# A fused recurrent attention and gated FFN: first v load in two halves, k and q ahead of v for two chunks, one attention block and its casts two groups later

## The chip, the cores and the metric

One core of a Trainium2 chip. The time is device microseconds (us) of one execution; most executions agree within a few tenths of a per cent, and the kernel before measured 230.6 to 232.7 us over four sets of rounds. "Faster" and "slower" mean a difference of more than 2%.

## The reference, cut to what matters

```python
gamma = 1.0 - 2.0 ** (-5.0 - np.arange(H))            # B, H, S, D = 4, 8, 768, 64
for t in range(S):
    state = gamma * state + k[t] outer v[t]            # per batch and head, 64 x 64
    y[t]  = scale * q[t] @ state
x   = y as (B*S, H*D)                                  # 3072 x 512
out = (sigmoid(x @ w_gate) * (x @ w_val)) @ w_out      # d_ff = 1536
```

## The kernel before

The sequence is cut in chunks of 128 tokens (six for each batch, 24 in all), and the recurrence becomes masked scores within a chunk plus a carried state. 512 tokens of x at a time then go through the FFN: 12 "up" groups (gate and value columns, the product into hT) and 8 "down" groups. In the second 512 tokens, where the change works, groups 0 to 7 are up groups for the first 256 tokens (each two sets of four matmuls of 128x256), and the "column groups" after them do the same for the other 256. Groups are counted from 0. Attention work for later chunks is put between the groups by a plan: after group i, do this step.

Chunks 0 to 3 are loaded as two runs of 256 tokens, k and q cast to bf16 by GpSimd's DMA, the first v by SyncE's:

```python
def load_run(x, a, dtype, eng, name):
    t = const.tile([128, H, 2 * D], dtype, name=name, tag=name, bufs=1)
    eng.dma_start(out=t, in_=x[0, :, a * 2 * C:(a + 1) * 2 * C, :].rearrange("h (p j) d -> p h (j d)", j=2))
    return t
vr[0] = load_run(v, 0, F32, nc.sync, "vr")
nc.scalar.preload_act_table(AX.Exp)
kr[0] = load_run(k, 0, BF16, nc.gpsimd, "kr0")
# ... qr[0], kr[1], qr[1] on GpSimd, later vr[1] on GpSimd, the weights, then chunks 4 to 9
```

Chunks 4 to 7 are transposed on TensorE (`step_t`: transposes, a ScalarE copy to qkT, VectorE's scaling of v). From chunk 8 on, SyncE transposes by DMA (qkX), and GpSimd's loads of chunks 10 and 11 wait for qkX of 8.

```python
def block(done, new):        # cut to its parts; new: the two chunks whose scores start; done: the two that are finished
    # inter(done): q @ carried state; scores(new); intra(done); state(new)   -- TensorE
    # y_out(done), masks(new), state_sum(new)                                -- VectorE
def casts(g):                # the carried state of g, g+1 to bf16           -- ScalarE
plan = {
    0: [(9, step_t, 4), (10, step_t, 5), (11, block, None, 4), (12, step_t, 6), (13, casts, 4), (13, step_t, 7),
        (14, block, 4, 6), (15, scale_v, 8)],
    1: [(0, casts, 6), (2, scale_v, 9), (4, block, 6, 8), (6, casts, 8), (10, scale_v, 10), ...,
        (12, block, 8, 10), ...],
# ... cut
```

Names in the profile lines: kn, qn, vf are a chunk's loads and vs the scaled v (kr, qr, vr, vsr for the runs of 256); za is the carried state and zbd its bf16 copy; ff is an accumulator of TensorE, gs the sigmoid, ob an output.

Each engine runs its instructions in program order, so a step also holds up what stands behind it on its engine.

Of the kernel before, what the change touches and what calls it, by code (L numbers as in the profile page):

```python
# [9 lines left out]
F32 = mybir.dt.float32  # L10
BF16 = mybir.dt.bfloat16
# [6 lines left out]
def kernel(  # L18
# [10 lines left out]
    nc = tc.nc  # L29
    B, H, S, D = q.shape  # L30
    N_TOK, D_MODEL = out.shape
    D_FF = moe_w_gate.shape[1]
    C = 128
# [25 lines left out]
    def load_v(g):  # L59
        vf[g] = ld.tile([C, H, D], F32, tag="vf", name="vf", bufs=6)  # L60
        nc.gpsimd.dma_start(out=vf[g], in_=src(v, g))  # L61

    def load_kq(g):
        kn[g] = ld.tile([C, H, D], BF16, tag="kn", name="kn")
        qn[g] = ld.tile([C, H, D], BF16, tag="qn", name="qn")
        nc.gpsimd.dma_start(out=kn[g], in_=src(k, g))  # L66
        nc.gpsimd.dma_start(out=qn[g], in_=src(q, g))  # L67

    def load_chunk(g):
        load_kq(g)  # L70
        load_v(g)


    def load_run(x, a, dtype, eng, name):
        t = const.tile([128, H, 2 * D], dtype, name=name, tag=name, bufs=1)
        eng.dma_start(out=t, in_=x[0, :, a * 2 * C:(a + 1) * 2 * C, :].rearrange("h (p j) d -> p h (j d)", j=2))
        return t

    wg = wpool.tile([128, KT, D_FF], BF16, name="wg")
# [9 lines left out]
    def load_out(s):  # L89
        nc.gpsimd.dma_start(out=wo[:, s * 3:(s + 1) * 3, :],  # L90
                            in_=moe_w_out.rearrange("(n p) d -> p n d", p=128)[:, s * 3:(s + 1) * 3, :])


    kr, qr, vr, vsr = {}, {}, {}, {}
    vr[0] = load_run(v, 0, F32, nc.sync, "vr")
    nc.scalar.preload_act_table(AX.Exp)
    kr[0] = load_run(k, 0, BF16, nc.gpsimd, "kr0")
    ident = const.tile([128, 128], BF16, name="ident")
    make_identity(nc, ident)
    ident4 = ident.unsqueeze(1).to_broadcast([128, 4, 128])  # L100
# [1 line left out]
    nc.gpsimd.iota(tokr, pattern=[[2 * C, 2], [1, 2]], base=0, channel_multiplier=2)  # L102
    tokv = const.tile([128, NCH], I32, name="tokv")
    nc.gpsimd.iota(tokv, pattern=[[C, NCH]], base=0, channel_multiplier=1)
    qr[0] = load_run(q, 0, BF16, nc.gpsimd, "qr0")
    toky = const.tile([128, 384], I32, name="toky")
    nc.gpsimd.iota(toky, pattern=[[1, 384]], base=0, channel_multiplier=0)
    kr[1] = load_run(k, 1, BF16, nc.gpsimd, "kr1")
    qr[1] = load_run(q, 1, BF16, nc.gpsimd, "qr1")

    lgh = const.tile([128, H], F32, name="lgh")
    for h in range(H):
# [39 lines left out]
    def bank(shape, dt=F32):  # L152
        return pf.tile(shape, dt, tag="ff", name="ff")
# [122 lines left out]
    def scale_run(a, eng):  # L276
        vsr[a] = const.tile([128, H, 2, D], BF16, name=f"vsr{a}")
        eng.tensor_tensor(vsr[a], runs(vr[a]), tabr[:, a].unsqueeze(3).to_broadcast([128, H, 2, D]), op=ALU.mult)  # L278
# [173 lines left out]

    make_taby(0)
    scale_run(0, nc.vector)
    vr[1] = load_run(v, 1, F32, nc.gpsimd, "vr")
    maskr = const.tile([128, 2, 2, D], F32, name="maskr")
    nc.gpsimd.memset(maskr, 1.0)
    for i in range(2):
# [51 lines left out]
    extend_taby(5)  # L510
    for s in range(4):
        load_out(s)
    for g in range(4, 8):
        load_chunk(g)
    y[3] = bank([128, NP, C])
    intra_run(1, [3])
    y_out_run(2)
# [15 lines left out]
    def downs(t):  # L533
# [2 lines left out]
    plan = {  # L536
        0: [(9, step_t, 4), (10, step_t, 5), (11, block, None, 4), (12, step_t, 6), (13, casts, 4), (13, step_t, 7),
            (14, block, 4, 6), (15, scale_v, 8)],
        1: [(0, casts, 6), (2, scale_v, 9), (4, block, 6, 8), (6, casts, 8), (10, scale_v, 10), (11, scale_v, 11),
            (12, block, 8, 10), (14, casts, 10), (16, scale_v, 12), (17, scale_v, 13), (20, block, 10, 12),  # L540
            (22, casts, 12)],
        2: [(3, scale_v, 14), (4, scale_v, 15), (6, block, 12, 14), (8, casts, 14), (11, scale_v, 16),
# [69 lines left out]
```

## Time and profile before

| | before |
|---|---|
| time, median of the first 3 runs | 231.94 us |
| span of the profiled run | 229.3 us |
| TensorE / VectorE / ScalarE / GpSimd busy | 96 / 51 / 38 / 34% |
| granted TensorE clock | 1.0 |
| TensorE idle in the span | 9.4 us, 3.0 of them before its first matmul |

TensorE is the bound, and only holes in its work can be won. "Idle before" in a profile line gives the time the engine stood and what ended it. Since ends of matmuls are modelled, starts are the surer reading. The lines are in the prediction.

I use five marks, 0 (the start of the span) and four starts on TensorE: B, the block of chunks 4 to 6; C, the first up group of the second 512 tokens; D, the block of chunks 8 to 10; E, the last matmul. Before: B 50.07, C 53.29, D 72.26, E 225.89 us.

### The profile page before, as it was taken

The numbers are of one execution on the slowest core, as the hardware profiler recorded it, in microseconds if no ns is written. First come the engines' busy times: TensorE is split into PE (matmuls) and PEld (weight loads), VectorE is DVE, ScalarE is ACT, GpSimd is POOL, SyncE is SP. The second block draws the span as 40 slices with busy tenths as digits, with TensorE's granted clock in tenths as the row PEclk, the third lists the DMA queues.
The fourth block names the chain that finished last, engine by engine and source line by source line (L and its number), as shares of the span: only waits on it lengthen the run. The fifth ranks groups of instructions, "written<-read, shape, count | busy, mean of one in ns | idle before, by whom it ended". The sixth has DMA issues, their size and how long they took to land.

```text
span 229.3 us, 4531 instructions
## 1 busy us (share of the span) xinstructions
PE 219.9 (96%) x1815; PEld 119.1 (52%) x1815; DVE 117.9 (51%) x224; ACT 87.0 (38%) x162; POOL 78.9 (34%) x106
## 2 busy tenths in 40 slices
PE   4879999999899999999999999999999999999994
PEld 1557544567687445445445445445445454444443
DVE  5586433459876927368626267637267520343301
ACT  5785332554362421632521532623432512433221
POOL 7899956740724417080620090810000000000000
PEclk9999999999999999999999999999999999999999
DMA  7999999999897999799792399992420012100022
GB/s 136 219 189 196 198 206 196 186 242 194 108 190 60 164 149 175 191 129 171 61 192 94 92 137 160 94 165 88 105 40 0 0 49 91 46 0 0 4 91 92
DMA packets 77653, 28.08 MB, mean 122 GB/s; under 512 B 64192, under 2 KB 73280, under 8 KB 77632
## 3 DMA queue, kind: packets, MB, share of 16 engines
q0 software_dynamic: 55440, 16.78, 65.3%
q1 hardware_dynamic: 22048, 10.95, 23.8%
q8 instruction: 14, 0.23, 0.4%
q10 hardware_dynamic: 144, 0.07, 0.1%
q14 instruction: 7, 0.06, 0.1%
HBM read 28.31 MB, written 6.29 MB: 151 GB/s over the span
## 4 chain that ended last, share of the span: by engine, by line
PE 84%; DMA 10%; POOL 2%; issue 1%; DVE 1%; SPq 1%; DVEq 0%
PE ff L386 47%; PE ff L422 23%; PE ff L404 5%; DMA kn<-in_k_dram 4%; DMA wv<-in_moe_w_val_dram 3%; PE ff L232 2%; PE ff L183 2%; DMA vr<-in_v_dram 2%; DMA qkX<-qn 2%; PE ff L195 1%; PE ff L441 1%; PE z L201 1%; DVE vsr L278 1%; SPq L169 1%; PE ff L162 0%
## 5 line engine op out<-in xcount | busy, mean ns | idle before, releaser
L393 DVE TENSOR_TENSOR hT<-gs,ff 128x512 bf16<-128x512 f32 (+1 forms) x70 | 44.8, 648 | 59.1 <-PE ff L386 53.4
L386 PE MATMUL ff<-xT,wg 128*128 128x512 bf16 (+1 forms) x280 | 67.6, 364 | 0.2 <-DVE hT L393 0.2
L386 PE MATMUL ff<-xT,wv 128*128 128x512 bf16 (+1 forms) x280 | 67.6, 364 | 0.1
L392 ACT ACTIVATE gs<-ff 128x512 f32<-128x512 f32 (+1 forms) x70 | 39.5, 567 | 67.7 <-PE ff L386 61.7
L422 PE MATMUL ff<-wo,hT 128*128 128x512 bf16 x276 | 62.2, 379 | 0.0
L386 PEld LDWEIGHTS <-wv 128*128 128x128 bf16 x280 | 27.3, 98 | 29.3 <-DMA wv<-in_moe_w_val_dram 0.3
L422 PEld LDWEIGHTS <-hT 128*128 128x128 bf16 x276 | 26.3, 98 | 30.5
L386 PEld LDWEIGHTS <-wg 128*128 128x128 bf16 x280 | 26.9, 98 | 28.3 <-issue 0.4
L427 ACT COPY ob<-ff 128x512 f32<-128x512 f32 x23 | 13.5, 585 | 49.2 <-PE ff L422 45.1
L250 DVE TENSOR_TENSOR xT<-ff,taby 128x512 bf16<-128x512 f32 x20 | 12.9, 686 | 22.7 <-PE ff L232 22.7
L553 POOL COPY gate<-qkX 1x1 bf16<-1x1 bf16 x7 | 1.6, 234 | 59.0 <-DMA qkX<-qn 59.0
L66 POOL DMA_DIRECT2D kn<-in_k_dram x20 | 17.9, 894 | 5.8 <-DMA qkX<-kn 1.5
L207 ACT CAST zbd<-za 64x256 bf16<-64x256 f32 x38 | 15.3, 403 | 10.1 <-DVE za L219 4.8
L67 POOL DMA_DIRECT2D qn<-in_q_dram x20 | 18.0, 899 | 2.7 <-DMA wo<-in_moe_w_out_dram 1.6
L61 POOL DMA_DIRECT2D vf<-in_v_dram x20 | 18.4, 918 | 1.5 <-DMA wo<-in_moe_w_out_dram 1.0
L174 DVE TENSOR_TENSOR vs<-vf,tabv 128x512 bf16<-128x512 f32 x20 | 13.6, 686 | 6.8 <-DMA vf<-in_v_dram 6.8
L188 DVE TENSOR_TENSOR stA<-ff,causal 128x512 bf16<-128x512 f32 x20 | 13.6, 681 | 0.0
L189 DVE TENSOR_TENSOR stB<-ff,causal 128x512 bf16<-128x512 f32 x20 | 13.6, 680 | 0.0
L404 PE MATMUL ff<-xT,wg 128*128 128x256 bf16 x56 | 7.3, 273 | 1.1 <-DMA wg<-in_moe_w_gate_dram 1.1
L433 PE MATMUL ff<-ident 128*128 128x512 bf16 x15 | 5.3, 494 | 3.0 <-POOL ident masks.py:199 3.0
L404 PE MATMUL ff<-xT,wv 128*128 128x256 bf16 x56 | 7.3, 273 | 0.1
L411 DVE TENSOR_TENSOR hT<-gs,ff 128x512 bf16<-128x512 f32 x7 | 4.7, 687 | 4.0 <-PE ff L404 3.9
(86 smaller groups left out, 150.0 us busy)
## 6 DMA issues: line engine op xcount, KB each, us to landing
out_dram<-ob SPq DMA_DIRECT2D x23, 256.0 KB, 2.1
vf<-in_v_dram POOLq DMA_DIRECT2D x20, 256.0 KB, 5.5
kn<-in_k_dram POOLq DMA_DIRECT2D x20, 128.0 KB, 4.9
qn<-in_q_dram POOLq DMA_DIRECT2D x20, 128.0 KB, 5.7
wg<-in_moe_w_gate_dram POOLq DMA_DIRECT2D x6, 256.0 KB, 7.6
wv<-in_moe_w_val_dram POOLq DMA_DIRECT2D x6, 256.0 KB, 8.3
wo<-in_moe_w_out_dram POOLq DMA_DIRECT2D x4, 384.0 KB, 10.1
vr<-in_v_dram SPq DMA_DIRECT2D x1, 512.0 KB, 4.2
```

The lines of the kernel that those rows point to most:

```text
L61: nc.gpsimd.dma_start(out=vf[g], in_=src(v, g))
L66: nc.gpsimd.dma_start(out=kn[g], in_=src(k, g))
L67: nc.gpsimd.dma_start(out=qn[g], in_=src(q, g))
L174: nc.vector.tensor_tensor(vs[g], vf[g], tabv[:, g % NCH, :].unsqueeze(2).to_broadcast([C, H, D]), op=ALU.mult)
L188: nc.vector.tensor_tensor(stA[g], sc[g][0], causal4, op=ALU.mult)
L189: nc.vector.tensor_tensor(stB[g], sc[g][1], causal4, op=ALU.mult)
L207: nc.scalar.copy(zbd[g % 4][half, :, half], z[half])
L386: nc.tensor.matmul(u[:, lo:hi], w[:, kk, n1 * 128:(n1 + 1) * 128], x_cols(t, kk, lo, hi), start=(kk == 0), stop=(kk == KT - 1))
L392: nc.scalar.activation(gs[:, lo:hi], ps[0][:, lo:hi], AX.Sigmoid)
L393: nc.vector.tensor_tensor(hT[t][:, n1, lo:hi], gs[:, lo:hi], ps[1][:, lo:hi], op=ALU.mult)
L404: nc.tensor.matmul(u[:, i * n:(i + 1) * n], w[:, kk, n1 * 128:(n1 + 1) * 128], x_cols(t, kk, lo, hi), start=(kk == 0 and (rows == 1 or i = ...
L422: nc.tensor.matmul(o, hT[t][:, n1, sm * 128:(sm + 1) * 128], wo[:, n1, :], start=(n1 == 0), stop=(n1 == NFF - 1))
```

## The change

The intent: get the first v sooner by splitting its load over two issuing engines; let q of chunk 7 land before v of 6 so that TensorE needn't wait for it; and move the block of 6 to 8 to a place where its DMA transposes have landed, with the casts of 6 behind two more sigmoids.

```diff
+            eng.dma_start(out=t[:, i * n:(i + 1) * n], in_=runs[:, i * n:(i + 1) * n])   # for each engine
...
-    vr[0] = load_run(v, 0, F32, nc.sync, "vr")
+    vr[0] = load_run(v, 0, F32, "vr", nc.sync, nc.scalar)
...
-    for g in range(4, 8):
-        load_chunk(g)
+    load_chunk(4)
+    load_chunk(5)
+    for load in (load_kq, load_v):
+        load(6)
+        load(7)
...
-        1: [(0, casts, 6), (2, scale_v, 9), (4, block, 6, 8), (6, casts, 8), (10, scale_v, 10), (11, scale_v, 11),
+        1: [(2, casts, 6), (3, scale_v, 9), (6, block, 6, 8), (9, casts, 8), (10, scale_v, 10), (11, scale_v, 11),
```

More of the change, by code (lines that the diff above doesn't have):

```diff
@@ L71, in load_chunk, with load_run @@
         load_v(g)
-    def load_run(x, a, dtype, eng, name):
+    def load_run(x, a, dtype, name, *engines):
         t = const.tile([128, H, 2 * D], dtype, name=name, tag=name, bufs=1)
-        eng.dma_start(out=t, in_=x[0, :, a * 2 * C:(a + 1) * 2 * C, :].rearrange("h (p j) d -> p h (j d)", j=2))
+        runs = x[0, :, a * 2 * C:(a + 1) * 2 * C, :].rearrange("h (p j) d -> p h (j d)", j=2)
+        n = H // len(engines)
+        for i, eng in enumerate(engines):
+            eng.dma_start(out=t[:, i * n:(i + 1) * n], in_=runs[:, i * n:(i + 1) * n])
         return t
@@ L94 @@
     kr, qr, vr, vsr = {}, {}, {}, {}
-    vr[0] = load_run(v, 0, F32, nc.sync, "vr")
+    vr[0] = load_run(v, 0, F32, "vr", nc.sync, nc.scalar)
     nc.scalar.preload_act_table(AX.Exp)
-    kr[0] = load_run(k, 0, BF16, nc.gpsimd, "kr0")
+    kr[0] = load_run(k, 0, BF16, "kr0", nc.gpsimd)
     ident = const.tile([128, 128], BF16, name="ident")
@@ L104 @@
     nc.gpsimd.iota(tokv, pattern=[[C, NCH]], base=0, channel_multiplier=1)
-    qr[0] = load_run(q, 0, BF16, nc.gpsimd, "qr0")
+    qr[0] = load_run(q, 0, BF16, "qr0", nc.gpsimd)
     toky = const.tile([128, 384], I32, name="toky")
     nc.gpsimd.iota(toky, pattern=[[1, 384]], base=0, channel_multiplier=0)
-    kr[1] = load_run(k, 1, BF16, nc.gpsimd, "kr1")
-    qr[1] = load_run(q, 1, BF16, nc.gpsimd, "qr1")
+    kr[1] = load_run(k, 1, BF16, "kr1", nc.gpsimd)
+    qr[1] = load_run(q, 1, BF16, "qr1", nc.gpsimd)
     lgh = const.tile([128, H], F32, name="lgh")
@@ L454 @@
     scale_run(0, nc.vector)
-    vr[1] = load_run(v, 1, F32, nc.gpsimd, "vr")
+    vr[1] = load_run(v, 1, F32, "vr", nc.gpsimd)
     maskr = const.tile([128, 2, 2, D], F32, name="maskr")
```

## The prediction

> **What bounds the kernel now.** I read the first two parts of the page (busy shares, the 40 slices), then TensorE's waits, then the chain of waits, then the order in time of TensorE, ScalarE, GpSimd and SyncE between 40 and 75 us, and last the packet and landing records of the DMA queues.
>
> ```profile
> PE 219.9 (96%) x1815; PEld 119.1 (52%) x1815; DVE 117.9 (51%) x224; ACT 87.0 (38%) x162; POOL 78.9 (34%) x106
> ...
> DMA  7999999999897999799792399992420012100022
> ```
>
> TensorE is busy in 219.9 of 229.3 us at full granted clock, so at most 9.4 us can be won, and 3.0 of those pass before its first matmul. The DMA line is near full to slice 15, about 86 us, then thins. So the change works on a few small holes in the first third. TensorE's own waits name them:
>
> ```profile
> PE ff L433 <- POOL ident masks.py:199: 3.0, 1, 3.0
> PE ff L404 <- DMA wg<-in_moe_w_gate_dram: 1.1, 1, 1.1
> PE ff L183 <- DMA qkX<-qn: 0.6, 1, 0.6
> PE ff L162 <- DMA qn<-in_q_dram: 0.3, 1, 0.3
> PE ff L386 <- DVE hT L393: 0.2, 1, 0.2
> ```
>
> The last three are the target of parts two and three. In order of time around the block of chunks 6 to 8:
>
> ```profile
> 48.54 0.40 PE L162 MATMUL ff<-ident,qn 128*128 128x128 bf16 x4 [0.31 <-DMA qn<-in_q_dram]
> ...
> 57.14 0.60 PE L386 MATMUL ff<-xT,wg 128*128 128x256 bf16 x4 [0.20 <-DVE hT L393]
> 57.84 0.60 PE L386 MATMUL ff<-xT,wv 128*128 128x256 bf16 x4
> 58.27 0.39 PE L195 MATMUL ff<-qkT,zbd 128*128 128x128 bf16 x4
> 58.71 0.40 PE L183 MATMUL ff<-qkX 64*128 64x128 bf16 x8
> 59.68 0.40 PE L183 MATMUL ff<-qkX 64*128 64x128 bf16 x8 [0.57 <-DMA qkX<-qn]
> ```
>
> Starts matter more than the bracketed idle, because ends are modelled. Undisturbed, a set of four 128x256 matmuls starts every 0.436 us (54.60, 55.03, 55.47 in the trace), the first part of the block takes 0.22 and each set of scores 0.27. The starts above are late by 0.36 (57.14; the set before started at 56.34), 0.26, 0.22 and 0.70: 1.54 us lost here, not the 0.8 that the brackets show. The first two losses have one cause:
>
> ```profile
> 55.73 1.65 ACT L207 CAST zbd<-za 64x256 bf16<-64x256 f32 x4 [1.36 <-DVE za L217]
> 57.40 1.31 ACT L392 ACTIVATE gs<-ff 128x256 f32<-128x256 f32 x4
> ```
>
> ScalarE stands at the casts of chunk 6 from 54.37 until za is there, and the sigmoids of groups 1 to 4 queue behind; TensorE lacks a free accumulator.
>
> **What the Trainium skill says.** "DMA: Bandwidth & Descriptors", section "Issuing engines are not separate DMA queues": DMAs from several engines run on the same 16 engines and interleave; starting them on several engines only saves sequencer time. The trace agrees in part. From 3.0 to 4.0 us v alone moves about 67 packets of 512 B per 0.1 us at 27 ns each, which is all 16 engines. But from 1.9 to 2.9 it moves only 12 to 19 per 0.1 us, so the engines starve and a second issuer might help there. Section "Queues, rings and completion order" of that page: each engine goes round-robin between rows, a whole packet of at most 64 descriptors at a time. v is 1024 packets, 64 for each engine, and kr (issued at 1.32) starts only as v ends: its first packets appear at 4.0 and its rate rises from 9 to 65 per 0.1 us while v's falls from 62 to 7. That fits a kr held behind v, though it does not prove it.
>
> **The change part by part.**
>
> **1. v in two halves.** Chain and GpSimd suggest that v matters:
>
> ```profile
> 0.81 4.23 DMA vr<-in_v_dram
> ...
> 6.65 0.89 POOL vr L76
> ...
> 9.55 6.55 DMA wv<-in_moe_w_val_dram
> ```
>
> The tempting reading is that v sooner frees GpSimd's next issue sooner (it idles 0.48 us for vsr), hence the weights sooner. I don't believe it: GpSimd's queue is full already. Its landings follow each other with no hole: kr 6.79, qr 8.22, kr 9.72, qr 11.21, second v 12.86, first wg 14.94, wv 16.10, then one 256 KB weight piece per 1.3 us. The second v is issued at 6.65 but its packets run only from about 10 to 11.6. An earlier issue just queues longer. (Only the first v is split, the second stays with GpSimd.) Nor does TensorE wait for vsr: it is done at 6.37 and first used at 7.40. What remains is a kr that starts sooner because v ends sooner. If two issuers double the slow start, about 170 more of the 1024 packets are moved by 2.9 us, worth 170/67 x 0.1 = 0.25 us at the full rate. The whole GpSimd queue would move by that, and with it TensorE, which waits for wg until 14.98 and for wv until 16.15. ScalarE has room: its table load ends at 2.09 and its next work is at 3.92. Estimate 0 to 0.4, taken as 0.2 us.
>
> **2. k, q of 6, 7 before v.** The number of issues and bytes is unchanged. q of chunk 7 landed at 48.49, after v of 6; as fourth rather than fifth of these six it lands about one piece (1 us) sooner, and TensorE's 0.31 us at 48.54 goes. v of 6 lands at about 48.3 instead of 46.13; VectorE then scales it by 49.1, still before v of 7 (49.45, scaled 50.2), and the state matmuls need both only at 51.6. Gain 0.31 us.
>
> **3. Casts and block later.** With the casts behind group 2 instead of group 0, ScalarE does the sigmoids of groups 1 and 2 before za is ready: the 0.26 goes. The 0.36 stays, since VectorE reaches hT of group 0 only at 56.67. The block then comes behind groups 5 and 6, which take 1.75 us together; TensorE reaches its scores at about 60.0, when qkX has landed (the last at 59.54): 0.22 and 0.70 go. One edge: groups 8 on read the second half of xT, which the block's y_out writes. By my count y_out ends near 62.05 and group 8 is reached at 62.2, so it just fits. About 0.1 us of other hitches is ignored. Gain 1.54 - 0.36 = 1.18, about 1.2 us.
>
> Sum on TensorE at 62 us: 0.2 + 0.31 + 1.2 = 1.7 us.
>
> **What is given back.** The next block reads the transposed q of chunk 11:
>
> ```profile
> 68.37 2.07 SPq L169 DMA_TRANSPOSE qkX<-qn  x1
> ...
> 72.26 0.61 PE L195 MATMUL ff<-qkX,zbd 128*128 128x128 bf16 x8
> 72.81 0.40 PE L183 MATMUL ff<-qkX 64*128 64x128 bf16 x8
> ```
>
> That transpose lands at 71.94. Its scores start near 72.97 (72.26 + 0.44 + 0.27), so the slack is about 1.0 us. The chain behind it (qkX of 8 landed 58.58, GpSimd's gate, loads of 10 and 11 from 59.15, transposes) hangs on the DMA queues, not on TensorE, so parts 2 and 3 don't bring it forward; part 1 would. Of the 1.5 us of parts 2 and 3 I expect 0.9 to 1.5 to survive: 0.5 is lost to a new wait at chunk 11's scores unless the transposes happen to run faster. They well may: both groups of transposes stall about 1.2 us (57.0 to 58.2, 69.5 to 70.5), each time just after a 16 KB instruction fetch of over 1 us, which moves with TensorE's progress. I take 1.05. From there on TensorE has no wait worth naming, so what is ahead stays ahead.
>
> **Rivals.** (a) All hidden: the 1.5 us is fully given back at the block of chunks 8 to 10, and v's split does nothing: 231.9. For it: the thin slack; against: the slack is positive, so about 1 us must survive. (b) The chain of waits is right and v's issue sets the weights: up to 0.5 us for GpSimd plus all of parts 2 and 3, nothing given back: about 229.9. Against: the gapless landings. (c) A new wait: v halves delay kr by taking two turns to its one, or VectorE's burst after the later block holds the column groups or casts of 8: 232 to 232.8. Against: v moves the same bytes, kr starts after it anyway, and the accumulators that the column groups need are freed about 0.2 us or more ahead.
>
> **Range and chances.** 0.2 + 1.05 = 1.25 us off 231.94 is 230.7. The three timed runs spread over 0.6 us, about as wide as the doubt about v (0.4) and about the giving back (0.6), so 229.8 to 231.8 should hold eight times in ten. Two per cent would be 4.6 us: no hole this change touches is that large, in either direction.
>
> **What would show it.** Right: no wait of TensorE at the transposes of 7 nor at the block of 6 to 8; that block starts near 59.5; kr's first packets and landing a little before 4.0 and 6.79; a new wait of up to 0.7 us, or none, at chunk 11's scores near 71 to 72. Wrong: kr's landing unmoved or later (part 1), a wait at the column groups for xT (part 3), or a block of 8 to 10 at the old time, which would leave nothing.

## The result, and the profile after

Median 229.89 us (229.68 to 230.38, 6 runs) against 231.30 us for the kernel before (230.77 to 232.09, 6 runs). Ratios here are the mean time of one kernel's fast runs over that of the other's of the same rounds, so not quite the ratio of the medians: 0.9937, 95% interval 0.9914 to 0.9960, or 1.46 us less between the means. By the 2% rule that is "the same"; by the interval it is a real gain of about 0.6%.

First the busy shares and the DMA line of the page after:

```profile
PE 220.3 (97%) x1815; PEld 119.4 (52%) x1815; DVE 117.9 (52%) x224; ACT 87.4 (38%) x162; POOL 78.6 (34%) x106
...
DMA  7999999999999999899892499992410012100022
```

The work is the same; only the span is shorter, 228.0 for 229.3 us. TensorE's waits after (us in total, times, longest):

```profile
PE ff L436 <- POOL ident masks.py:199: 3.0, 1, 3.0
PE ff L407 <- DMA wg<-in_moe_w_gate_dram: 0.7, 1, 0.7
PE ff L269 <- DMA qr<-in_q_dram: 0.4, 1, 0.4
PE ff L407 <- DMA wv<-in_moe_w_val_dram: 0.3, 1, 0.3
```

The waits for q of 7, for qkX and for hT are gone from this list. Those for the first loads and weights remain. (The kernel before also had three short waits in the first 13 us, for kr and stB, that the prediction's list leaves out.) In order of time around the moved block (start us, us):

```profile
48.55 0.39 PE L165 MATMUL ff<-ident,qn 128*128 128x128 bf16 x4
...
50.61 0.85 PE L186 MATMUL ff<-qkT 64*128 64x128 bf16 x16
...
57.01 0.60 PE L389 MATMUL ff<-xT,wg 128*128 128x256 bf16 x4
57.44 0.60 PE L389 MATMUL ff<-xT,wv 128*128 128x256 bf16 x4
...
59.63 0.39 PE L198 MATMUL ff<-qkT,zbd 128*128 128x128 bf16 x4
59.95 0.67 PE L186 MATMUL ff<-qkX 64*128 64x128 bf16 x16
```

From C (53.51) every start follows in the undisturbed step of 0.437 us, through all seven groups into the block. The scores of 6 and 7 at 50.61, though, took 0.85 us. In the kernel before the same line took 0.62, which is 0.23 us less:

```profile
50.61 0.62 PE L183 MATMUL ff<-qkT 64*128 64x128 bf16 x16
```

That is a new wait; experiment 2 comes back to it. ScalarE in the same stretch:

```profile
55.96 0.39 ACT L395 ACTIVATE gs<-ff 128x256 f32<-128x256 f32 x1 [0.49 <-PE ff L389]
56.37 1.65 ACT L210 CAST zbd<-za 64x256 bf16<-64x256 f32 x4
58.04 0.94 ACT L395 ACTIVATE gs<-ff 128x256 f32<-128x256 f32 x3
```

It does the sigmoid of group 2 first, and the casts no longer wait for za. At the block of 8 to 10, where the prediction expected something to be given back:

```profile
67.84 1.19 SPq L172 DMA_TRANSPOSE qkX<-qn  x1
...
71.05 0.61 PE L198 MATMUL ff<-qkX,zbd 128*128 128x128 bf16 x8
71.59 0.62 PE L186 MATMUL ff<-qkX 64*128 64x128 bf16 x16
```

No wait, but only just: the transposed q of 11 landed at 71.66 us, and its scores started at 71.83, 0.17 us later. Where TensorE did wait for such a transpose (before and experiments 1, 2, 5, 7 and 10), it started 0.13 to 0.14 us after the landing, so the slack was about 0.03 us. The moved block itself had none: q of 9 landed at 60.08, its scores started at 60.22, 0.27 us behind those of 8 where 0.23 is undisturbed (experiment 3). It still lost about 0.04 us. At the start of the kernel the chain of waits reads almost as before:

```profile
0.81 4.19 DMA vr<-in_v_dram
...
6.60 0.89 POOL vr L79
...
9.51 6.87 DMA wv<-in_moe_w_val_dram
```

By the marks, before against after: 0 to B 50.07 and 50.06 us; B to C 3.22 and 3.45; C to D 18.98 and 17.54; D to E 153.63 and 153.63. The gain of the profile, 1.21 us, is the 1.44 won between C and D less the 0.23 lost between B and C; from D on nothing changed by as much as 0.01 us. Inside the first stretch two things cancel: the first full up group started 0.28 us later (24.29 for 24.01), and the way from there to B was 0.29 us shorter.

### The profile page after: what moved, and what is told of

Same layout as the page of the kernel before. It is cut to its first block, busy times and chain, and to the rows that moved or that the text cites. A ratio compares the mean times of both kernels' runs of the same rounds, so it can differ in the third digit from the quotient of the medians.

```text
span 228.0 us, 4533 instructions
## 1 busy us (share of the span) xinstructions
PE 220.3 (97%) x1815; PEld 119.4 (52%) x1815; DVE 117.9 (52%) x224; ACT 87.4 (38%) x162; POOL 78.6 (34%) x106
## 4 chain that ended last, share of the span: by engine, by line
PE 90%; DMA 5%; POOL 1%; ACT 1%; DVE 1%; issue 0%; DVEq 0%
PE ff L389 50%; PE ff L425 26%; PE ff L407 5%; DMA wv<-in_moe_w_val_dram 3%; PE ff L235 2%; PE ff L186 2%; DMA vr<-in_v_dram 2%; PE ff L198 1%; PE ff L444 1%; PE z L204 1%; PE ff L165 1%; DVE vsr L281 1%; ACT qkT L167 0%; POOL vr L79 0%; POOL maskr L463 0%; ACT zbd L210 0%
## 5 line engine op out<-in xcount | busy, mean ns | idle before, releaser
L436 PE MATMUL ff<-ident 128*128 128x512 bf16 x15 | 5.8, 532 | 3.0 <-POOL ident masks.py:199 3.0
```

## The experiments

Experiments 1 to 4 ran on one chip in one set of rounds; 5 to 12 ran on another chip, in three sets. Each set had its own runs of the kernel before, but 12 shares those of 9 to 11 and adds one. Means below are of 5 or 6 runs against 11 or 12.

**1. Only v in two halves (e1_v_split).**

```diff
-    vr[0] = load_run(v, 0, F32, nc.sync, "vr")
+    vr[0] = load_run(v, 0, F32, "vr", nc.sync, nc.scalar)
```

> Only v of the first two chunks in two halves. Theory A (v's end moves kr only a little, and the GpSimd queue's own pace hides it): kr's first packets up to 0.2 us earlier, its landing within 0.2 us of the kernel before, time within 0.3 us of it. Theory B (the chain through v sets the first weights): wg lands 0.3 to 0.5 us sooner and the time falls by 0.3 to 0.5 us. Theory C (the halves disturb the queue, as the profile of the whole change could suggest, where wg and wv land 0.07 and 0.28 us later than before): time up by 0.2 to 0.4 us.

Measured: ratio 0.9985 (0.9968 to 1.0003), 0.30 us less and not clear of nothing. The packet records explain why little can come of it (packets that started in each 0.1 us, by issuer):

```
us      before, SyncE    halves: SyncE  ScalarE
2.1          19                45         0
2.5          18                11         0
2.9          37                40        26
3.5          70                29        37
last v     4.41 us            4.30 us
first kr   4.00 us            3.95 us
```

ScalarE's half was issued at the same time (0.81 us), but its first packet came at 2.78 us, 0.85 after SyncE's; from 3.0 both share the rate that one had. v ends 0.1 us sooner and kr starts 0.05 us sooner. Two profiles can mislead here, so take all: by 3.0 us the three with the split (after, 1, 9) had started 275 to 328 packets, the ten with v in one piece by SyncE 179 to 281, with means of 302 and 217. That lead of 85 packets ends v about 0.1 us sooner (last packets at 4.28 to 4.38 against 4.36 to 4.53 us), but kr's first packet (3.85 to 3.95 against 3.81 to 4.08) and its landing (6.51 to 6.71 against 6.22 to 7.42) are not sooner beyond their scatter. Theory A holds for the mechanism. B's landings of the weights did not show: wg landed at 15.78 us, later than the 14.94 of before. The cause of that is elsewhere: the sixteenth completion of the second k came at 11.46 us, 1.27 us after the fifteenth. Such a late last part came and went from profile to profile, with and without the split (0.02 to 1.39 us among thirteen profiles), so C is not shown by it either.

**2. Only k, q of 6 and 7 before v (e2_kq_order).**

```diff
-    for g in range(4, 8):
-        load_chunk(g)
+    load_chunk(4)
+    load_chunk(5)
+    for load in (load_kq, load_v):
+        load(6)
+        load(7)
```

> Only k, q of chunks 6, 7 ahead of their v. Theory A (the wait for q of 7 goes, but ScalarE's copy of the transposes of 7 stands behind an output copy and the casts of 4, so the scores of 7 wait in its place): no wait at the transposes of 7, a wait of about 0.2 us at the scores of 7, and less than 0.15 us of the 0.31 us kept; at the block of 6 to 8 that gain is lost again, because it waits for the transposes from the DMA, so the time is within 0.2 us of before. Theory B (the hole is simply removed): time down by 0.3 us.

Measured: ratio 0.9976 (0.9958 to 0.9994), 0.57 us less between the means. Its profile shows the first part of theory A; first TensorE, then ScalarE, in order of time:

```profile
48.26 0.39 PE L162 MATMUL ff<-ident,qn 128*128 128x128 bf16 x4
...
50.32 0.84 PE L183 MATMUL ff<-qkT 64*128 64x128 bf16 x16
```
```profile
48.24 0.59 ACT L427 COPY ob<-ff 128x512 f32<-128x512 f32 x1 [0.27 <-PE ff L422]
48.85 0.82 ACT L207 CAST zbd<-za 64x256 bf16<-64x256 f32 x2
49.69 1.02 ACT L164 ACTIVATE qkT<-ff 128x1024 bf16<-128x1024 bf16 x1
```

No wait at the transposes of 7; but their copy by ScalarE stands behind an output copy and the casts of 4 and ends at 50.71, while TensorE reached the scores of 7 at 50.59. They start 0.22 us late (B to C 3.44 for 3.22). What the order wins is the old hole minus 0.22 us. The old hole itself varies with how the start of the kernel went. The next transposes of q of 7 come 1.74 us after those of 6 if nothing waits, and came after 2.22, 1.91, 2.02, 2.30, 1.74 and 1.85 us in the six profiles with the old order (before, 1, 3, 5, 6, 7). The second part of A (all lost at the next block) did not hold: C to D was 18.74, 0.24 us less than before, since the transposes of 9 landed at 59.23 for 59.54. But experiment 1, with the old order and the old plan, had 18.55 there, so that 0.24 can't be put down to the order. By the profiles the order is worth 0 to 0.3 us, and the 0.57 of the totals, with an interval of 0.14 to 0.97, doesn't settle it further.

**3. Only the plan (e3_plan).**

```diff
-        1: [(0, casts, 6), (2, scale_v, 9), (4, block, 6, 8), (6, casts, 8), (10, ...
+        1: [(2, casts, 6), (3, scale_v, 9), (6, block, 6, 8), (9, casts, 8), (10, ...
```

> Only the later casts and the block of 6 to 8 two groups later. Theory A (this part is nearly the whole gain): no wait in TensorE from the first up group of the second 512 tokens to the block of 8 to 10, the distance from the start of that first group to the start of the block of 8 to 10 falls from 18.97 us to about 17.5, time down by 1.2 to 1.5 us. Theory B (half of the gain or more is due to the other two parts): time down by 0.7 us or less, with a wait left at the block.

Measured: ratio 0.9926 (0.9908 to 0.9944), 1.67 us less; C to D 17.49 us, no wait between them. Theory A: this part alone gives what the whole change gives.

**4. The whole change without the split (e4_no_v_split).** The edits of 2 and 3 together.

> The whole change without the split of v. Theory A (the split is worth nothing): time equal to the whole change within 0.2 us, that is 1.2 to 1.7 us below before. Theory B (the split is worth 0.2 to 0.5 us): only 0.9 to 1.2 us below before. Theory C (the split costs): 1.7 us or more below before.

Measured: ratio 0.9917 (0.9897 to 0.9938), 1.87 us less; C to D 17.50, B to C 3.44. That is theory C's range by the number, but only 0.2 us below the plan alone, within the noise. The split is not needed for the gain; whether it costs was left to 9 and 10.

**5. Only the casts of 6 later (e5_casts_only), the block in its old place.**

```diff
-        1: [(0, casts, 6), (2, scale_v, 9), (4, block, 6, 8), (6, casts, 8), (10, ...
+        1: [(2, casts, 6), (3, scale_v, 9), (4, block, 6, 8), (6, casts, 8), (10, ...
```

> Only the casts of 6 (and the scaling of v of 9) later, the block of 6 to 8 where it was. Theory A (two causes in a row; with the first removed TensorE only comes to the second sooner): the late starts of the fourth up group of the second 512 tokens (0.36 and 0.26 us) are gone, but the scores of the block wait that much longer for the transposes of 8 and 9, whose landing does not move: 1.3 to 2 us of waiting there, time within 0.3 us of before. Theory B (the casts alone are most of the gain): time down by 0.6 us or more.

```profile
56.94 0.60 PE L386 MATMUL ff<-xT,wg 128*128 128x256 bf16 x4
57.38 0.60 PE L386 MATMUL ff<-xT,wv 128*128 128x256 bf16 x4
57.82 0.39 PE L195 MATMUL ff<-qkT,zbd 128*128 128x128 bf16 x4
58.13 0.67 PE L183 MATMUL ff<-qkX 64*128 64x128 bf16 x8
59.88 0.40 PE L183 MATMUL ff<-qkX 64*128 64x128 bf16 x8 [1.08 <-DVE hT L393]
```

The late starts are gone, the block is reached 0.61 us sooner after C (4.37 for 4.98 us), and the second set of scores starts 1.48 us later than it could (59.88 for 58.13 + 0.27). C to D: 19.02 us, against 18.98 before. All 0.61 us are given back, as theory A said. The profile puts the wait down to VectorE's hT, which ended near the same time; but q of 9 landed at 59.74, 0.14 before the start, and in the kernel before at 59.54, 0.14 before its start, so the transposes would have held it there in any case. In all five profiles with the block in its old place (before, 1, 2, 5, 7) the scores of 9 start 0.13 to 0.14 us after that landing. The total is 0.44 us less (ratio 0.9975, 0.9954 to 0.9997), more than the 0.3 expected; in the profile, which is of the slowest of the six runs (231.17 us), that difference isn't between C and D, and its cause stays open.

**6. Only the block later (e6_block_only), the casts of 6 in their old place.**

```diff
-        1: [(0, casts, 6), (2, scale_v, 9), (4, block, 6, 8), (6, casts, 8), (10, ...
+        1: [(0, casts, 6), (2, scale_v, 9), (6, block, 6, 8), (9, casts, 8), (10, ...
```

> Only the block of 6 to 8 two groups later (with its casts of 8), the casts of 6 where they were. Theory A: no wait at the scores of the block, but late starts of about 0.6 us in the up groups stay, since ScalarE still stands at the casts; time 0.8 to 1.1 us below before. Theory B (the block's place is all that counts): 1.4 to 1.7 us below before, no late starts in the up groups.

```profile
57.22 0.60 PE L386 MATMUL ff<-xT,wv 128*128 128x256 bf16 x4
58.01 0.60 PE L386 MATMUL ff<-xT,wg 128*128 128x256 bf16 x4 [0.19 <-DVE hT L393]
58.71 0.60 PE L386 MATMUL ff<-xT,wv 128*128 128x256 bf16 x4
```

Starts 0.79 and 0.70 us apart instead of 0.44: 0.35 + 0.26 = 0.61 us late, as before, and no wait at the block. C to D 18.11 us, 0.87 less. Total 0.71 us less (0.9967, 0.9943 to 0.9990), a little under what theory A gave; the profile is A's. So, by one profile each, the two halves of the plan are worth 0 and 0.87 us singly, and 1.48 together: the casts pay only once the block no longer waits.

**7. A probe: v on GpSimd's queue behind k and q (e7_v_behind_q).**

```diff
-    vr[0] = load_run(v, 0, F32, nc.sync, "vr")
     qr[0] = load_run(q, 0, BF16, nc.gpsimd, "qr0")
+    vr[0] = load_run(v, 0, F32, nc.gpsimd, "vr")
```

> A probe, meant to be slower: v of the first two chunks is issued by GpSimd behind k and q, so that no transfer of a hardware queue stands beside the first k. Theory A (k is held behind v on the same engines): k's first packets come at about 3.0 us instead of 4.0, and it lands about 1 us sooner. Theory B (k starts when its own queue is ready, and that it starts as v ends is chance): first packets still at 3.8 to 4.0 us, landing within 0.2 us of 6.2 to 6.8.

Measured: one run of 236.29 us, as expected slower: v landed at 10.54 us for 5.04, GpSimd issued wg at 14.28 for 8.78, and wg landed at 20.73 for 14.94, so a v that is late enough does hold the weights back. k's first packet came at 3.03 us, where the thirteen other profiles have 3.81 to 4.08. Theory A: k is held behind v. But k landed at 5.73 us, only 0.5 us sooner than in the best of the others (6.22), because from 3.0 to 3.9 it ran at only 8 to 26 packets per 0.1 us, as slowly as v does in its first microsecond. In this one run the slow start went to k, once k came first. Whether that is what kept the second issuer from doing more for v is not shown.

**8. A version meant to beat both: no split, casts of 4 one group sooner (e8_casts4_early).** To the kernel of experiment 4:

```diff
-(12, step_t, 6), (13, casts, 4), (13, step_t, 7),
+(12, casts, 4), (12, step_t, 6), (13, step_t, 7),
```

> A version meant to beat both: the new order of k, q and the new plan, v in one piece, and the casts of 4 one group sooner, so that ScalarE copies the transposes of 7 about 0.8 us sooner. Theory A (the scores of 7 wait only for that copy): the wait of about 0.23 us at the scores of 7 is gone, time 0.1 to 0.3 us below the version without the split of v (which was 1.9 us below before), unless the scores of 11, which had only 0.3 us to spare, take it back. Theory B: no change beyond 0.1 us, with a new wait at the scores of 11.

Measured: B to C 3.22 us, so the 0.22 us at the scores of 7 are gone: the casts of 4 were what held ScalarE's copy up. The total is unclear: ratio 0.9947 (0.9915 to 0.9980), runs from 228.94 to 231.24 us.

**9 to 11. The whole change, without the split, and with the casts of 4 sooner, on one chip (e9_whole, e10_no_v_split_again, e11_casts4_early_again).** Same kernels as after, 4 and 8.

> The whole change, on one chip with the version without the split of v. Theory A (the split of v is worth nothing either way, the new order of k, q next to nothing): 1.3 to 1.8 us below before, within 0.3 us of the version without the split. Theory C (the split costs about 0.4 us, as the ratios on two chips could suggest): 0.3 to 0.5 us above the version without the split.

> The whole change without the split of v, a second time, on one chip with the whole change. Theory A: 1.3 to 1.9 us below before and within 0.3 us of the whole change. Theory C: 0.3 to 0.5 us below the whole change.

> The version with the casts of 4 one group sooner, a second time (its first run spread over 2.3 us), beside the same kernel without that step. Theory A (the 0.22 us at the scores of 7 are kept): 0.1 to 0.4 us below the version without it, at best just outside the noise. Theory B (the first run's mean was right and something is given back): level with or above that version; then a new wait shows in the profile between the block of 4 to 6 and the block of 8 to 10.

| | mean us | ratio to before (95%) | B to C | C to D | D to E |
|---|---|---|---|---|---|
| 9 whole change | 230.01 | 0.9950 (0.9922 to 0.9979) | 3.44 | 17.50 | 153.62 |
| 10 without the split | 229.88 | 0.9944 (0.9915 to 0.9973) | 3.44 | 17.65 | 154.42 |
| 11 casts of 4 sooner | 229.40 | 0.9927 (0.9898 to 0.9956) | 3.22 | 17.50 | 153.62 |

9 and 10 differ by 0.13 us, so the split neither wins nor costs anything that can be seen; theory C fell. Both gained 1.1 to 1.2 us, less than the 1.3 expected; the kernel before had two runs above 231.6 us and most near 230.7 here. The profile of 10 shows what the prediction had feared:

```profile
70.44 0.61 PE L195 MATMUL ff<-qkX,zbd 128*128 128x128 bf16 x8
71.37 0.40 PE L183 MATMUL ff<-qkX 64*128 64x128 bf16 x8 [0.31 <-DMA qkX<-qn]
72.00 0.40 PE L183 MATMUL ff<-qkX 64*128 64x128 bf16 x8 [0.24 <-DMA qkX<-qn]
```

In this execution TensorE came to the block of 8 to 10 at 70.44 us, 0.6 sooner than in 9, but q of 11 landed only at 71.87. It lost 0.80 us there (D to E 154.42 for 153.62), and 0.15 before it, at the scores of 9 in the moved block (C to D 17.65 for 17.50; they started 0.14 us after q of 9 landed). 11 is 0.48 us below 10 in this set, but with its first run (8) pooled the mean is 229.74, only 0.14 below 10. I take the 0.22 us in the profiles as shown and its effect on the total as likely, no more.

**12. The block of 8 to 10 one group later as well (e12_block8_later).** To the kernel of 11:

```diff
-            (12, block, 8, 10), (14, casts, 10),
+            (13, block, 8, 10), (15, casts, 10),
```

> The version with the casts of 4 sooner, and the block of 8 to 10 (with its casts) one group later. In one profile of the version without the split TensorE waited 0.5 us at that block for the transposes of 10 and 11, in the others it passed with 0.2 to 0.3 us to spare. Theory A (this is the giving back that the prediction feared, and it strikes in some executions): the scores of 11 now have about 2 us to spare, no wait there, time 1.5 to 2.1 us below before. Theory B (the later block brings a wait of its own, for accumulators or for the casts of 10 at the block of 10 to 12): time 1.0 us or less below before, with that wait in the profile.

Measured: mean 229.29, median 229.20 us, ratio 0.9920 (0.9890 to 0.9950), 1.86 us below before. The scores of 11 started at 72.99, q of 11 had landed at 70.43. C to D plus D to E is 171.12 us, the same 171.12 as in 11, so in this profile the later block costs nothing, and the scores of 11 have 2.4 us of slack. No new wait: theory A. This version is 0.7 us below the whole change on the same chip, the lowest mean of all, though 11 and 12 can't be told apart by their totals.

## Why the prediction was right or wrong

The time was right: 1.25 us less predicted, 1.46 measured, and 229.89 us lies inside the range. Its terms were less so, and partly made up for each other: in the profile they came to 0 for v, -0.23 between B and C, 1.44 for the plan and nothing given back, 1.21 in all, against 0.2, 0.31, 1.18 and -0.45. There is luck in the total too. The prediction subtracts from 231.94 us, the median of the first three runs; all six had 231.30. And 229.89 is the number of rival (b), "about 229.9", of which only "nothing given back" came true in the profile: the weights landed no sooner.

**The bound and the size of the holes: right.** The late starts, not the bracketed 0.8 us, are what was won: 1.48 us between C and D in experiment 3, 1.44 in the whole change. The prediction's 1.54 is a little high, since it takes 0.22 us for the first part of the block where the profiles without a wait have 0.32 (59.63 to 59.95 after). Experiments 3, 5 and 6 confirm both parts: 0.61 us from the casts, the rest from the transposes.

**Part 1, the split of v: wrong in size, nothing to be seen for 0.2 us.** The steps that failed are "If two issuers double the slow start" and, after it, "a kr that starts sooner because v ends sooner". The split had about 85 packets more started by 3.0 us, half of the 170 that the prediction had by 2.9, and it ended v some 0.1 us sooner; the second half's packets came only 0.65 to 0.85 us after the first's. kr's first packet and landing moved no further than they scatter without the split. (Its "12 to 19" packets per 0.1 us are 6 to 19 in the trace.) The signs that it named, kr's first packet "a little before 4.0" and its landing before 6.79, came (3.85 and 6.71), but kernels with v in one piece show them as well. The reading that an earlier issue by GpSimd wins nothing was not contradicted: wg was issued 0.25 us sooner in 9 than before, and landed at 14.27 us, inside the 13.93 to 15.92 of the ten with v in one piece. The step before, k held behind v, was right; one profile shows it (7).

**Part 2, the order: the hole went, but a part came back.** The step that failed is "Gain 0.31 us": it checked VectorE's scaling and the state matmuls, but not ScalarE's copy of the same transposes, which stands behind the casts of 4. That puts 0.22 us back at the scores of 7 in every profile where nothing waited at the transposes of 7 (after, 2, 4, 9 and 10, and 6, which has the old order); where the casts of 4 come sooner (8, 11, 12) it is gone.

**Part 3, casts and block: mechanism right, term too small, 1.44 for 1.18 us** (0.61 for 0.26 from the casts, 0.83 for 0.92 from the block). The step that failed is "The 0.36 stays, since VectorE reaches hT of group 0 only at 56.67". VectorE did reach it no sooner (56.90 after), yet group 4 started on time at 57.01, while that product was still being made. The wait records show the accumulators dealt in another order: the second matmul set of group 3 waits for VectorE in the kernel before, and for ScalarE in the changed one. With the casts behind the sigmoids, a buffer freed by ScalarE is taken there, and group 0's product is not waited for. The records and starts of experiment 5 (casts alone) are the new ones, those of 6 (block alone) the old, so it is the casts that decide; that the order of the accumulators is the way is read from the records, not tested. The edge at xT held with nothing to spare: y_out ended at 62.29, the column groups started at 62.34.

**The giving back: right as a risk, absent from the profile of the changed kernel.** The prediction's "0.5 is lost to a new wait at chunk 11's scores unless the transposes happen to run faster" met the second case: q of 11 landed 0.28 us sooner than before, and just in time. Its "slack is about 1.0 us" left out the 0.14 us from a landing to the start of a waiting matmul. In experiment 10 the first case came: 0.80 us. So it is a race that falls one way or the other from execution to execution, and in the profile of 12 it is out of the way.

**Downstream: right.** D to E was 153.62 or 153.63 us in all profiles but that of 10 and, with its block moved, 12. What is ahead at the block of 8 to 10 stays ahead.

**What stays open.** The first loads of the kernel end at different times in each execution, by up to 1.4 us for one transfer; TensorE's start of the block of 4 to 6 lies between 49.35 and 50.79 us in the thirteen profiles other than the probe's. Which DMA engine is late, and why, the records don't tell. That noise is as large as parts 1 and 2, which is why their totals settle nothing.

## What to carry to other kernels

When two waits stand in a row on the bounding engine, removing the first alone may show nothing, and removing the second alone only its own part; test them singly and together before dropping either. Before counting a hole as won, walk every in-order queue between it and the next user of the same data, and also note how close behind it the next transfer lands, and add the time from landing to start (0.14 us here): what then has a few hundredths to spare may wait in the next execution. Splitting one early load over two issuers moved nothing here, where the DMA queue behind it was already full.

## What the Trainium skill lacked or had wrong

- "DMA: Bandwidth & Descriptors", sections "Issuing engines are not separate DMA queues" and "Rules for kernel authors": that spreading DMAs over engines doesn't help bandwidth holds here (9 against 10: 0.13 us). Lacking: of two halves issued at the same time by SyncE and ScalarE, ScalarE's began 0.65 to 0.85 us after SyncE's (first packets at 1.93, and at 2.58, 2.62 and 2.78 us). ScalarE also loads its activation table until 2.61 us in that stretch; whether that has a part in it was not tested.
- Same page, "Queues, rings and completion order": switching only at packet boundaries, after 64 descriptors at most, fits what was seen (the 9 to 17 that it calls typical hardly: k should then have begun at about 3.0 us, in turns with v), but the cost isn't given: GpSimd's k, 64 descriptors for each engine behind 64 of v, started at 3.8 to 4.1 us instead of 3.03 (experiment 7).
- No page that I used has the slow start of the first transfer: 6 to 19 packets of 512 B per 0.1 us in its first microsecond (kernel before), then about 67.
- Same page, "Why a DMA increments its semaphore by 16 and not by 1": it says that only the full 16 count. Lacking is how far apart they come: the sixteenth followed the fifteenth by 0.02 to 1.39 us for the same transfer (the second k) in thirteen profiles.
- No page that I used has this: in both main profiles each of the three 16 KB instruction fetches that fell among the DMA transposes (56.5, 68.9 and 82.1 us before; 57.5, 68.7 and 81.2 after) was followed within 0.4 to 0.7 us by transpose packets that took 1.4 us instead of about 0.02. That is a coincidence in time, seen six times of six; no run here tested it. Packets of up to 2.0 us also came from 54.0 us on in both, with no such fetch near, so the fetch can't be the only cause.
